# Order, spacing and queues of the last output stores of an attention and MLP kernel

## The chip, the core and the metric

The kernel runs on one core of a Trainium2 chip. Its time is the device time of one execution in microseconds (us), measured on the chip. The engines are TensorE (PE in the profile; its weight loads are shown apart as PEld), VectorE (DVE), ScalarE (ACT), GpSimd (POOL) and SyncE (SP), which here only issues transfers (DMAs). Each engine works through its own queue in order and waits at semaphores for the others. "Issue" of a DMA is the time its engine spends on starting it; it "lands" later, when the last of its 16 completion counts has arrived.

## What is computed

The input x has 2048 rows of 512. It is normalised row by row, goes through an attention with 32 heads of 16 that works in four segments of 512 rows and carries a memory from segment to segment, and through an MLP with a hidden width of 1792. Both results are added to x.

```python
xn = _layernorm(x, axis=-1)
return x + _A_ref(xn, A_wq, A_wk, A_wv, A_wo, A_beta) + _B_ref(xn, B_w1, B_w2)

# _A_ref, for each segment s (qs, ks, vs: its 512 rows, per head)
p = _softmax(logits, axis=-1)                 # causal within the segment
a_dot = jnp.einsum('bhqk,bhkd->bhqd', p, vs)
num = jnp.einsum('bhld,bhde->bhle', pq, M)    # pq = phi(qs), M and z from earlier segments
den = jnp.einsum('bhld,bhd->bhl', pq, z)[..., None] + 1e-06
o = g * (num / den) + (1.0 - g) * a_dot       # all heads together, then o @ wo

# _B_ref
h = _silu(jnp.einsum('bsd,df->bsf', x, w1))
out = jnp.einsum('bsf,fd->bsd', h, w2)
```

## The kernel before

All five engines run from one order written out by hand: the string ORDER (lines 16 to 98) is a list of words, and the loop at line 795 turns each word into the instructions of one piece of work, in that order. Each engine's queue gets its instructions in the order of the words. PIECES (line 759) says which function a word calls. The words that matter here, with s the segment (0 to 3), are:

- S (line 653): a batch of attention scores and their exponentials, the last being S78; E and O (line 687) weigh the values, Ev and Oa copy the results out of PSUM (lines 716 and 722). Oa issues four small DMAs that carry sums of the weights to the tile zraw and four that complete the tile oraw (lines 708 and 730).
- R, W (lines 519 and 527): reciprocals of the sums, for the last segment in two parts; r, w do this for the memory's sums.
- z and d (lines 548 and 558): two DMAs each that spread such reciprocals over all rows (spread, line 536, issue at 542). zv and dv multiply by them, n is a product with the memory's state (line 566), nv adds it and completes one of four slices of the tile oT (line 570).
- o3.j.i (line 593): one product of output tile j (128 rows of 512) of the last segment with contraction step i. Steps 0 to 13 take the MLP's hidden tile hT and w2, steps 14 to 17 take the four slices of oT and wo. oc is half of such a product in columns, od a quarter. Eighteen steps complete a tile.
- oh.i.h (line 625): the same for tile 3 of the last segment, which is made in two halves of 256 columns, each in a PSUM bank of its own. Tile 2 and the two halves lie in one PSUM tile of four banks (fin, an instance of psS), which is free when the last scores have been read. Tiles 0 and 1 have a bank each from the pool pb, which has four.
- st3.j (line 639, store at 581): when all products of a tile are in, VectorE forms 0.5 times the sum plus the residual row tile (line 586) and SyncE stores the 128 KB result (line 591). sh.h (line 628) does it for a half of tile 3, 64 KB (lines 633 and 637). These are called output passes below.
- xl3.j (line 576): SyncE loads the residual tile of x that the pass adds (line 579).

A product has two forms (line 317): whole, one matmul of 128 output rows, or narrow, four matmuls of 32 output rows each that run side by side. The loop chooses by what stands ahead, so that TensorE does not change its form too often; after the last scores all products are narrow.

TensorE works in the order of the words, so a tile's pass comes as soon as its last product is in and VectorE reaches it. The order of the five last passes is tile 0, half 0, tile 2, tile 1, half 1. All stores of the kernel go out from SyncE's queue, in which the spreads, the moves and the residual loads stand too. The pass of tile 1 of segment 2 (st2.1) stands in S78 ahead of the last weighing. ScalarE issues four DMAs in the whole kernel, all of them loads: two of x at the start, w2 and wo.

Of the kernel before, what the change touches and what calls it, by code (L numbers as in the profile page):

```python
# [91 lines left out]
S73 h3.2.1 ha3.2 Ev14 oc2.2.5.1 o2.1.2 o2.2.16 o2.1.6 hv3.12 h3.8.0 o2.2.10 st2.2 hv3.2 o2.1.1 o2.1.5 h3.8.1 ha3.8 hv3.8  # L92
S79 o2.1.0 O14 Ov14 od2.1.12.2 s3 sv3 r3.1 o2.1.7 r3.3 h3.7.0 r3.2 r3.0 oc2.1.10.0 od2.1.12.3 o2.1.3 w3
S77 h3.6.0 R0.0 oc2.1.11.0 h3.7.1 R0.1 ha3.7 h3.6.1 hv3.7 d3.2 o2.1.14 R0.3 h3.9.0 ha3.6 hv3.6 o2.1.15
S76 o2.1.8 d3.0 d3.1 h3.9.1 o2.1.9 oc2.1.10.1 h3.13.0 ha3.9 od2.1.12.0 oc2.1.11.1 h3.13.1 xl3.3 hv3.9 o3.0.12 od2.1.12.1 o2.1.4 o3.0.1 o2.1.13 ha3.13
S75 dv3.2 R0.2 W0 o3.0.7 hv3.13 o3.0.4 h3.10.0 z3.2 o2.1.16 h3.10.1 z3.1 o3.0.2 o3.0.8 dv3.0 o3.0.9 o3.0.0 z3.0 ha3.10 hv3.10
S78 o3.0.5 h3.11.0 o2.1.17 st2.1 h3.11.1 E15 o3.0.6 o3.2.1 oh1.1 o3.1.8 Ev15 ha3.11 oc3.0.3.1 oh0.1 O15 oh12.1 o3.2.3 o3.2.5 hv3.11 zv3.1 oh5.1 o3.2.8 n3.2 Oa15 oh13.0 o3.1.3 o3.1.12 dv3.1 zv3.2 nv3.2 o3.2.7 oc3.0.11.1 oc3.0.11.0 oh9.0 n3.0 oh16.0 n3.1 zv3.0 o3.2.9 o3.1.1 oc3.1.0.1 o3.1.13 o3.2.0 oc3.1.0.0 o3.2.12 o3.2.6 nv3.0 od3.1.11.2 nv3.1 oh11.1 o3.1.14 oh15.1 o3.2.11 oh0.0 R1.1 R1.0 oh10.0 o3.0.14 od3.0.10.2 oh8.0 od3.1.11.3 d3.3 oh15.0 od3.0.10.0 R1.3 o3.1.6 R1.2 oc3.1.9.0 oc3.1.9.1 o3.1.5 oh2.0 o3.1.10 W1 oh14.0 o3.2.13 oh1.0 o3.1.15 oh5.0 o3.0.15 o3.0.16 dv3.3 z3.3 od3.0.10.1 o3.2.15 xl3.1 o3.2.16 zv3.3 o3.2.2 n3.3 oh11.0 od3.1.11.1 oh3.1 oh10.1 oh6.0 oh4.1 nv3.3 o3.1.4 od3.0.10.3 oh4.0 oh12.0 o3.2.4 o3.0.13 oc3.0.3.0 oh3.0 o3.0.17 xl3.0 st3.0 o3.2.14 od3.1.11.0 oh7.0 o3.2.17 oh17.0 oh7.1 sh0 o3.2.10 o3.1.2 oh2.1 o3.1.7 o3.1.16 st3.2 o3.1.17 oh17.1 st3.1 oh6.1 oh13.1 oh14.1 oh16.1 oh8.1 oh9.1 sh1
"""


# [1 line left out]
def kernel(  # L102
# [13 lines left out]
    nc = tc.nc  # L116

    P = 128
# [3 lines left out]
    NT = S // P  # L122
# [11 lines left out]
    out_flat = out.flatten_outer_dims()  # L134
# [40 lines left out]
    def load_w(eng, w_sb, W, k0, k1):  # L175
# [11 lines left out]
        out=beta_r[:], in_=bass.AP(tensor=A_beta.tensor, offset=A_beta.offset, ap=[[1, H], [0, 4], [1, 1]])  # L187
# [9 lines left out]
    for i in range(2):  # L197
# [6 lines left out]
        out=b16[:], in_=ones8[:], compare_op=ALU.is_ge, fill=0.0,  # L204
# [3 lines left out]
        out=b16[:], in_=b16[:], compare_op=ALU.is_ge, fill=0.0,  # L208
# [271 lines left out]
    LAST = NSEG - 1  # L480
# [100 lines left out]
    def store(s, j):  # L581

        st = sts[s]
        t = s * TPS + j
        o_out = work.tile([P, D], BF16, name="o_out", bufs=3)
        out = nc.vector.scalar_tensor_tensor(  # L586
            out=o_out[:], in0=st.pop(("psO", j)), scalar=0.5, in1=st["x", j][:], op0=ALU.mult, op1=ALU.add
        )
        if s == LAST and j >= 2:
            fin_out.append(((j,), out))  # L590
        nc.sync.dma_start(out=out_flat[t * P : (t + 1) * P, :], in_=o_out[:])

    def out_mm(s, j, i, half=None, part=0, parts=1):

# [33 lines left out]
    def half_store(h):  # L628

        st, j, cols = sts[LAST], TPS - 1, slice(h * D // 2, (h + 1) * D // 2)  # L630
        assert len(st.pop(("done", j, h))) == 4 * (FT + DT)
        o_half = work.tile([P, D // 2], BF16, name="o_half", bufs=2)
        out = nc.vector.scalar_tensor_tensor(
            out=o_half[:], in0=st["psO", j, h], scalar=0.5, in1=st["x", j][:, cols], op0=ALU.mult, op1=ALU.add
        )
        fin_out.append(((j, h), out))
        nc.sync.dma_start(out=out_flat[(NT - 1) * P : NT * P, cols], in_=o_half[:])

    def out_store(s, j):
        assert len(sts[s].pop(("done", j))) == 4 * (FT + DT)  # L640
        store(s, j)
# [111 lines left out]
    def keep_busy(n):  # L753
# [20 lines left out]
        "o": out_mm, "oh": half_out,  # L774
        "oc": lambda s, j, i, c: out_mm(s, j, i, None, c, 2), "od": lambda s, j, i, c: out_mm(s, j, i, None, c, 4),
        "sh": half_store, "xl": load_res, "st": out_store,
        "xs": ln_stats, "xc": ln_sums, "xd": ln_var, "xg": ln_root, "xq": ln_sqrt, "xi": ln_inv, "tb": first_exp,
        "Nv": lambda t: ln_norm(t, nc.vector), "Na": lambda t: ln_norm(t, nc.gpsimd),
# [55 lines left out]
```

## Time and profile before

| what | value |
|---|---|
| time, median of 3 runs | 228.55 us (228.1 to 229.02) |
| time of the profiled execution | 229.09 us |
| span of the profiled execution, first to last instruction | 227.4 us |
| TensorE busy | 217.2 us, 96% |
| ScalarE busy | 198.0 us, 87% |
| VectorE busy | 177.7 us, 78% |
| GpSimd busy | 113.9 us, 50% |
| stores of 128 KB (line 591) | 15, issued 87.3 to 224.0 us after the start |
| last issues of a residual load (line 579) | 217.56 us and 218.06 us |
| issues of SyncE between 196.8 and 218.5 us | 34 DMAs |

The profile is of one execution. A row of a timeline names the start, the duration, the engine, the line, the operation and the tiles, written as output<-input, and how many instructions are merged in it; what stands in brackets is the idle time ahead of it and what ended it. A busy TensorE is one with a matmul in flight; the ends of matmuls are modelled. The view by stage gives the busy time of each engine in a stretch, with its instructions, the granted clock (1.00 is full speed) and the share of the DMA engines. The chain of waits goes back from the end, at each step to what released it.

### The profile page before, as it was taken

The page shows a single profiled execution, that of the slowest core. Times are in us where ns is not written, and L with a number is a line of the kernel's source. Part 1 is how long each engine was busy: PE and PEld are TensorE (multiplying, and loading weights), DVE is VectorE, ACT ScalarE, POOL GpSimd, SP SyncE. Part 2 cuts the span into 40 slices and gives each one's busy share as a digit, 9 for nine tenths or more (in the row PEclk, how much of TensorE's full clock was granted, in tenths as well). Part 3 has the DMA queues.
Part 4 walks back from the last instruction along what each step waited for, and adds up shares of the span by engine and source line. Part 5 has one row for each costly group of instructions (what it writes and reads, how often), then busy time and mean ns, then how long its engine had stood idle before and what let it go on. Part 6 is the DMA issues. An engine that isn't in the chain of part 4 may idle for free.

```text
span 227.4 us, 7543 instructions
## 1 busy us (share of the span) xinstructions
PE 217.2 (96%) x3124; PEld 112.9 (50%) x3152; DVE 177.7 (78%) x351; ACT 198.0 (87%) x179; POOL 113.9 (50%) x173
## 2 busy tenths in 40 slices
PE   8999999999999999999999999999999999999993
PEld 8666645545534434444444434445444444445662
DVE  5799899987787897658798798747676888887834
ACT  3799998999999999999999899999999989897000
POOL 6059647667454673665644577546474265342000
PEclk9999999999999999999999999999999999999999
DMA  6992429323215213404314212141032212024122
GB/s 181 361 381 68 77 52 299 60 55 57 61 22 158 72 35 47 96 15 112 41 40 113 75 53 58 35 117 42 22 100 66 88 36 84 29 63 130 29 90 94
DMA packets 34787, 20.55 MB, mean 90 GB/s; under 512 B 15680, under 2 KB 34240, under 8 KB 34752
## 3 DMA queue, kind: packets, MB, share of 16 engines
q1 hardware_dynamic: 32128, 17.45, 28.3%
q10 hardware_dynamic: 2624, 2.62, 3.6%
q8 instruction: 24, 0.39, 0.8%
q14 instruction: 11, 0.09, 0.1%
HBM read 9.96 MB, written 2.10 MB: 53 GB/s over the span
## 4 chain that ended last, share of the span: by engine, by line
PE 62%; ACT 11%; DVE 11%; DMA 8%; issue 4%; SPq 2%; POOL 0%; DVEq 0%
PE ps L322 18%; PE psO L322 14%; PE psS L662 9%; ACT Pb L669 8%; PE ps L324 8%; PE psO L324 6%; PE psV L696 6%; DMA x_hi<-in_A_x_dram 4%; DMA spr<-rz 3%; ACT th L457 2%; DMA x_res<-in_A_x_dram 2%; DVE stats L272 1%; DVE o_out L586 1%; DVE kT L361 1%; PE psM L324 1%
## 5 line engine op out<-in xcount | busy, mean ns | idle before, releaser
L669 ACT ACTIVATE Pb<-psS 128x2048 bf16<-128x2048 f32 x80 | 150.2, 1878 | 5.8 <-PE psS L662 5.1
L677 POOL TENSOR_SCALAR_AFFINE_SELECT Pb<-Pb 128x512 bf16<-128x512 bf16 (+1 forms) x112 | 80.1, 729 | 85.1 <-ACT Pb L669 83.7
L462 DVE SCALAR_TENSOR_TENSOR hT<-th,ps 128x512 bf16<-128x512 bf16 x56 | 37.8, 679 | 14.1 <-ACT th L457 13.7
L322 PE MATMUL ps<-xnT,w_sb 128*128 128x512 bf16 (+1 forms) x177 | 43.3, 340 | 0.8 <-issue 0.5
L322 PE MATMUL psO<-w_sb,hT 128*128 128x512 bf16 (+2 forms) x139 | 36.1, 340 | 0.7 <-issue 0.5
L457 ACT ACTIVATE th<-ps 128x512 bf16<-128x512 f32 x56 | 32.8, 597 | 0.5 <-PE ps L322 0.4
L324 PE MATMUL psO<-w_sb,hT 128*32 128x128 bf16 (+2 forms) x468 | 26.7, 300 | 0.0
L322 PEld LDWEIGHTS <-w_sb 128*128 128x128 bf16 x184 | 17.1, 98 | 16.3 <-issue 3.3
L696 PE MATMUL psV<-Pb,Vz 128*32 128x128 bf16 (+3 forms) x512 | 23.1, 300 | 0.4 <-DVE oT L573 0.2
L322 PEld LDWEIGHTS <-hT 128*128 128x128 bf16 x149 | 13.6, 97 | 16.9 <-issue 4.8
L324 PE MATMUL ps<-xnT,w_sb 128*32 128x512 bf16 (+1 forms) x384 | 21.8, 329 | 0.0
L324 PEld LDWEIGHTS <-hT 128*32 128x32 bf16 x636 | 15.7, 97 | 9.7 <-issue 1.7
L696 PEld LDWEIGHTS <-Vz 128*32 128x32 bf16 x512 | 13.0, 96 | 10.6 <-issue 1.4
L662 PE MATMUL psS<-qT,kT 16*128 16x128 bf16 (+3 forms) x256 | 17.3, 301 | 0.9 <-ACT Pb L669 0.8
L662 PE MATMUL psS<-qT,kTo 32*128 32x384 bf16 (+3 forms) x256 | 17.2, 299 | 0.6 <-ACT Pb L669 0.2
L362 POOL TENSOR_SCALAR kTo<-kT,pm_odd 128x512 bf16<-128x512 bf16 x16 | 11.9, 747 | 8.2 <-DVE kT L361 7.3
L322 PE MATMUL ps<-xnT,wk_sb 128*128 128x512 bf16 (+1 forms) x66 | 15.4, 328 | 0.7 <-issue 0.5
L322 PE MATMUL ps<-wv_sb,xnT 128*128 128x512 bf16 x48 | 14.3, 380 | 0.6 <-issue 0.2
L662 PEld LDWEIGHTS <-kT 16*128 16x128 bf16 x256 | 5.9, 91 | 16.7 <-issue 16.2
L361 DVE CAST kT<-ps 128x512 bf16<-128x512 f32 x15 | 10.2, 687 | 4.6 <-PE ps L322 4.3
L586 DVE SCALAR_TENSOR_TENSOR o_out<-psO,x_res 128x512 bf16<-128x512 f32 x14 | 9.6, 687 | 5.3 <-PE psO L322 2.8
L719 DVE CAST oraw<-psV 128x512 bf16<-128x512 f32 x16 | 11.0, 688 | 3.4 <-PE psV L696 3.3
(105 smaller groups left out, 298.3 us busy)
## 6 DMA issues: line engine op xcount, KB each, us to landing
spr<-rz SPq DMA_DIRECT2D x56, 64.0 KB
x_res<-in_A_x_dram SPq DMA_DIRECT2D x16, 128.0 KB
out_dram<-o_out SPq DMA_DIRECT2D x15, 128.0 KB
w_sb<-in_B_w_dram SPq DMA_DIRECT2D x1, 1792.0 KB
w_sb<-in_B_w_dram ACTq DMA_DIRECT2D x1, 1792.0 KB
x_hi<-in_A_x_dram SPq DMA_DIRECT2D x2, 512.0 KB
oraw<-odd SPq DMA_DIRECT2D x64, 16.0 KB
wv_sb<-in_A_wv_dram SPq DMA_DIRECT2D x2, 256.0 KB
```

What stands on the lines that cost most here:

```text
L322: return [nc.tensor.matmul(out, lhsT=lhsT, rhs=rhs, start=start, stop=stop, skip_group_check=True)]
L324: nc.tensor.matmul(out[c : c + 32], lhsT=lhsT[:, c : c + 32], rhs=rhs, start=start, stop=stop, tile_position=(0, c), skip_group_check=True,)
L361: copy(out=kT[:, dt, :], in_=sts[s].pop(("k", dt))[:, :])
L362: nc.gpsimd.tensor_scalar(out=kTo[:, dt, :], in0=kT[:, dt, :], scalar1=pm_odd[:, 0:1], scalar2=1.0, op0=ALU.mult, op1=ALU.mult,)
L457: nc.scalar.activation(out=th[:], in_=sts[s]["h", ft][:, :], func=AF.Tanh, scale=0.5)
L462: nc.vector.scalar_tensor_tensor(out=st["hT"][:, ft, :], in0=st.pop(("th", ft))[:], scalar=1.0, in1=st.pop(("h", ft))[:, :], op0=ALU.add, ...
L586: out = nc.vector.scalar_tensor_tensor(out=o_out[:], in0=st.pop(("psO", j)), scalar=0.5, in1=st["x", j][:], op0=ALU.mult, op1=ALU.add)
L662: nc.tensor.matmul(psS[:, g, c0 : c0 + nq], lhsT=kk[rows, dt, kt * P : (kt + 1) * P], rhs=st["qT"][rows, dt, kt * P : L], start=True, stop ...
L669: exp = nc.scalar.activation(out=Pb[:, :, :], in_=psS[:, :, :], func=AF.Exp, scale=SCALE)
L677: mask = nc.gpsimd.affine_select(out=blocks, in_=blocks, compare_op=ALU.is_ge, fill=0.0, base=0, pattern=[[0, blocks.shape[1]], [1, P]], c ...
L696: nc.tensor.matmul(psV[32 * g : 32 * g + 32, kt * P : L], lhsT=Vzs[s % 2][:, kt, 4 * dt + g, par : par + 2, :].rearrange("p a d -> p (a d) ...
L719: copy(out=oraw[:], in_=sts[s].pop(("psV", 0))[:, :])
```

## The change

Two issue calls choose their queue, and the order of the last section is written anew. Nothing is computed in another way, and each product of the last segment is still formed once.

- The store of tile 2 of the last segment and the store of half 0 of tile 3 are issued from ScalarE's queue and not from SyncE's.
- The order of the five last passes becomes half 1, half 0, tile 0, tile 2, tile 1. Products of tile 1 fill the end: after half 1's pass come one product of tile 2 and then only products of tile 1 (a half, a quarter and four whole ones, and at last another half).
- Products of the halves (oh) begin earlier and end earlier. The MLP's hidden tiles 10 and 11 (h3.10, h3.11) come earlier by some words. The last slice of oT (d3.3, z3.3, n3.3, nv3.3) keeps its chain, but n3.3 stands nearer to the first product that reads it.
- st2.1 moves from ahead of the last weighing (E15) to after the last spread's issue: its store now stands in SyncE's queue between the residual loads of tiles 1 and 0.
- The reciprocals R1 stand ahead of nv3.1 and not behind it in VectorE's queue.

```diff
 S77 h3.6.0 R0.0 oc2.1.11.0 h3.7.1 R0.1 ha3.7 h3.6.1 hv3.7 d3.2 o2.1.14 R0.3 h3.9.0 ha3.6 hv3.6 o2.1.15
-S76 o2.1.8 d3.0 d3.1 h3.9.1 o2.1.9 oc2.1.10.1 h3.13.0 ha3.9 od2.1.12.0 oc2.1.11.1 h3.13.1 xl3.3 hv3.9 o3.0.12 od2.1.12.1 o2.1.4 o3.0.1 o2.1.13 ha3.13
-S75 dv3.2 R0.2 W0 o3.0.7 hv3.13 o3.0.4 h3.10.0 z3.2 o2.1.16 h3.10.1 z3.1 o3.0.2 o3.0.8 dv3.0 o3.0.9 o3.0.0 z3.0 ha3.10 hv3.10
-S78 o3.0.5 h3.11.0 o2.1.17 st2.1 h3.11.1 E15 o3.0.6 o3.2.1 oh1.1 o3.1.8 Ev15 ha3.11 oc3.0.3.1 oh0.1 O15 oh12.1 o3.2.3 o3.2.5 hv3.11 zv3.1 oh5.1 o3.2.8 n3.2 Oa15 oh13.0 o3.1.3 o3.1.12 dv3.1 zv3.2 nv3.2 o3.2.7 oc3.0.11.1 oc3.0.11.0 oh9.0 n3.0 oh16.0 n3.1 zv3.0 o3.2.9 o3.1.1 oc3.1.0.1 o3.1.13 o3.2.0 oc3.1.0.0 o3.2.12 o3.2.6 nv3.0 od3.1.11.2 nv3.1 oh11.1 o3.1.14 oh15.1 o3.2.11 oh0.0 R1.1 R1.0 oh10.0 o3.0.14 od3.0.10.2 oh8.0 od3.1.11.3 d3.3 oh15.0 od3.0.10.0 R1.3 o3.1.6 R1.2 oc3.1.9.0 oc3.1.9.1 o3.1.5 oh2.0 o3.1.10 W1 oh14.0 o3.2.13 oh1.0 o3.1.15 oh5.0 o3.0.15 o3.0.16 dv3.3 z3.3 od3.0.10.1 o3.2.15 xl3.1 o3.2.16 zv3.3 o3.2.2 n3.3 oh11.0 od3.1.11.1 oh3.1 oh10.1 oh6.0 oh4.1 nv3.3 o3.1.4 od3.0.10.3 oh4.0 oh12.0 o3.2.4 o3.0.13 oc3.0.3.0 oh3.0 o3.0.17 xl3.0 st3.0 o3.2.14 od3.1.11.0 oh7.0 o3.2.17 oh17.0 oh7.1 sh0 o3.2.10 o3.1.2 oh2.1 o3.1.7 o3.1.16 st3.2 o3.1.17 oh17.1 st3.1 oh6.1 oh13.1 oh14.1 oh16.1 oh8.1 oh9.1 sh1
+S76 o2.1.8 d3.0 d3.1 h3.9.1 o2.1.9 oc2.1.10.1 h3.13.0 ha3.9 od2.1.12.0 oc2.1.11.1 h3.13.1 xl3.3 hv3.9 o3.0.12 ha3.13 o3.0.8 R0.2 o2.1.17 o3.0.6 o3.0.2 o2.1.4
+S75 o3.0.9 h3.11.0 hv3.13 h3.10.0 o2.1.16 h3.10.1 o2.1.13 o3.0.0 oc3.0.3.0 ha3.10
+S78 od2.1.12.1 W0 h3.11.1 z3.0 dv3.0 o3.0.1 hv3.10 E15 o3.0.4 ha3.11 od3.0.10.1 dv3.2 oc3.0.3.1 z3.1 z3.2 Ev15 o3.0.13 o3.0.5 oh4.0 o3.2.12 oh0.0 oh2.1 hv3.11 zv3.0 oh5.1 od3.0.10.0 O15 dv3.1 oh3.1 oh7.1 n3.0 zv3.1 oh6.1 o3.2.13 Oa15 oh6.0 oh12.0 od3.0.10.3 o3.1.13 d3.3 o3.1.1 nv3.0 o3.1.8 oh3.0 n3.2 od3.0.10.2 o3.2.10 oh0.1 o3.1.3 zv3.2 o3.2.8 oh8.0 nv3.2 R1.1 oh13.1 oh10.1 od3.1.11.1 o3.0.7 oh16.0 R1.2 oh16.1 oh14.0 oc3.1.9.1 R1.3 R1.0 oh14.1 oh13.0 oh2.0 o3.1.16 o3.1.12 oh9.0 o3.2.0 o3.1.10 o3.2.7 oh1.1 n3.1 oh5.0 o3.1.2 oh10.0 o3.1.6 o3.1.4 W1 o3.2.9 oh12.1 nv3.1 oc3.1.0.1 z3.3 xl3.1 oh7.0 od3.1.11.0 o3.0.14 o3.2.14 oh8.1 oc3.0.11.0 st2.1 dv3.3 zv3.3 o3.0.16 o3.2.4 o3.2.11 o3.2.2 oh11.0 oh15.0 oh9.1 n3.3 oh15.1 xl3.0 o3.1.5 oh11.1 oh4.1 nv3.3 o3.2.15 oh1.0 o3.0.15 oh17.1 od3.1.11.2 o3.2.16 oh17.0 oc3.0.11.1 o3.2.1 o3.2.3 o3.0.17 o3.2.5 o3.2.17 sh1 o3.2.6 o3.1.15 oc3.1.9.0 od3.1.11.3 sh0 o3.1.7 st3.0 o3.1.17 o3.1.14 st3.2 oc3.1.0.0 st3.1
...
-        nc.sync.dma_start(out=out_flat[t * P : (t + 1) * P, :], in_=o_out[:])
+        (nc.scalar if s == LAST and j == 2 else nc.sync).dma_start(out=out_flat[t * P : (t + 1) * P, :], in_=o_out[:])
...
-        nc.sync.dma_start(out=out_flat[(NT - 1) * P : NT * P, cols], in_=o_half[:])
+        (nc.sync if h else nc.scalar).dma_start(out=out_flat[(NT - 1) * P : NT * P, cols], in_=o_half[:])
```

## The prediction

> **What bounds the kernel now.** I read the busy time by stage first, because the change acts on the end alone. Up to the word o3.0.12 of the order the instruction streams are the same; what differs starts near 203 us.
>
> ```profile
> core 0: us, PE busy (x) PEld busy (x) DVE busy (x) ACT busy (x) POOL busy (x), PEclk, DMA share, GB/s
> 210.00:215.00 5.00, 5.00 (x128) 3.12 (x120) 4.21 (x10) 0.59 (x1) 0.00 (x0) 1.00 0.16 43
> 215.00:220.00 5.00, 5.00 (x148) 3.45 (x144) 2.52 (x7) 0.00 (x0) 0.00 (x0) 1.00 0.37 111
> 220.00:223.50 3.50, 3.50 (x96) 2.30 (x88) 1.98 (x5) 0.00 (x0) 0.00 (x0) 1.00 0.06 18
> 223.50:227.40 3.90, 0.10 (x4) 0.00 (x0) 0.80 (x2) 0.00 (x0) 0.00 (x0) 1.00 0.38 122
> ```
>
> TensorE works without a hole at full clock until 223.5, then 3.9 us pass in which it does nothing. So the time is TensorE's stream plus that tail. The timeline of TensorE gives the stream's pace and two places that matter below:
>
> ```profile
> 218.49 0.39 PE L324 MATMUL ps<-phiQT,Mbf 128*32 128x512 bf16 x4
> 220.44 0.39 PE L324 MATMUL psO<-wo_sb,oT 128*32 128x512 bf16 x4
> 223.21 0.39 PE L324 MATMUL psS<-w_sb,hT 128*32 128x256 bf16 x8
> ```
>
> A product (four matmuls side by side in the narrow form) starts 0.216 us after the one before at 512 columns, 0.109 at 256, 0.056 at 128; a 512-column one is done 0.39 us after its start, a 256-column one 0.28 (starts and ends in this timeline). From 203 us on, the starts leave these intervals only at the four edges of the two last score batches, by about 0.1 us each. The last product starts at 223.32 and is done at 223.60. VectorE, SyncE's queue and the chain of waits give the tail:
>
> ```profile
> 219.53 0.69 DVE L573 TENSOR_TENSOR oT<-ps,oT 128x512 bf16<-128x512 f32 x1
> 221.75 0.69 DVE L586 SCALAR_TENSOR_TENSOR o_out<-psO,x_res 128x512 bf16<-128x512 f32 x1 [1.52 <-PE psS L324]
> 222.35 0.41 DVE L633 SCALAR_TENSOR_TENSOR o_half<-psS,x_res 128x256 bf16<-128x256 f32 x1
> 222.69 0.68 DVE L586 SCALAR_TENSOR_TENSOR o_out<-psS,x_res 128x512 bf16<-128x512 f32 x1
> 223.28 0.68 DVE L586 SCALAR_TENSOR_TENSOR o_out<-psO,x_res 128x512 bf16<-128x512 f32 x1
> 223.88 0.41 DVE L633 SCALAR_TENSOR_TENSOR o_half<-psS,x_res 128x256 bf16<-128x256 f32 x1
> ```
>
> ```profile
> 217.56 0.93 SPq L579 DMA_DIRECT2D x_res<-in_A_x_dram  x2
> 222.47 0.34 SPq L591 DMA_DIRECT2D out_dram<-o_out  x1
> 222.91 0.38 SPq L637 DMA_DIRECT2D out_dram<-o_half  x1
> 223.41 0.92 SPq L591 DMA_DIRECT2D out_dram<-o_out  x2
> 224.77 0.34 SPq L637 DMA_DIRECT2D out_dram<-o_half  x1
> ```
>
> ```profile
> 218.06 3.60 DMA x_res<-in_A_x_dram
> 221.75 0.53 DVE o_out L586
> 222.35 0.41 DVE o_half L633
> 222.77 1.19 DVE o_out L586 x2
> ```
>
> Read together: the first output pass waited for its residual load, which landed at 221.65, 3.60 us after issue; its neighbour of the same size took 2.26. From then on the five passes follow each other with no hole (0.60 us from start to start for a full one, 0.33 for a half), so VectorE and not TensorE ends the work: the last pass starts 0.28 us after its product is done and ends at 224.30. Its store is issued only at 224.77, although SyncE was free at 224.33. By the completion counts in the trace it lands at 226.53; the end follows 0.85 later, at 227.38. The tail after the last product's start is thus 0.98 (to the end of the pass) + 0.47 (to the issue) + 1.76 (to landing) + 0.85 = 4.06.
>
> **The change part by part.**
> *TensorE's amount of work.* The order holds the same products; three matmuls fewer (one product falls into the whole form). The same score batches, so the same four edges. Cost 0, as long as TensorE never waits (first rival).
>
> *The passes closed in the order half 1, half 0, tile 0, tile 2, tile 1.* The pass of half 1 waits for the product just ahead of it in the order, o3.2.17 (it lies in the same PSUM tile). Up to the last product (tile 1's, 256 columns) come then o3.2.6 and six products of tile 1, so o3.2.17 starts 6 x 0.216 + 0.109 + 0.056 = 1.46 us before that one, itself counted. With the stream's end where it is, it starts at 223.32 - 1.46 = 221.86 and is done at 222.25; the pass starts about 0.05 later (the row at 207.60 starts 0.03 behind its product, others to 0.05), at 222.30. Behind it, at VectorE's own pace: half 0 at 222.63, tile 0 at 222.96, tile 2 at 223.56, tile 1 at 224.16; it ends at 224.84. Tile 1's product is done at 223.60, so VectorE binds again, by 0.5 us: one half pass that stood last has become a full one, and it starts later. Against 224.30 this is +0.54. The residual loads hide: the last wanted one is now read at 222.96, so the 1.3 us by which one came late has cover; without the cover it was worth about 0.25 here.
>
> *The last store's issue.* The 0.37 us in which SyncE stood free ahead of its last store has two like it in its own stream, 0.45 near 71.4 and 0.39 near 150.6, and the three lie 128 SyncE instructions apart. With two stores and two waits gone to ScalarE, the last store stands two places ahead of the next such place, and the hole falls behind it, where SyncE waits for landings anyway. So the issue follows the pass by 0.03, as with tile 1's store at 223.99: 224.87 instead of 224.77. The two bounds are 0 and 0.37 for the hole; I take 0, by the equal distances. The Trainium skill (Runtime: NRT & Kernel Launch, Instruction fetch mechanics) says that instructions come in 16 KiB blocks of 256 and that crossing a boundary is mostly hidden; by that nothing would happen at 128, and the hole would be something else that may stay. The trace shows 8,192-byte packets of the instruction queue and a distance of 128, so I go by the trace.
>
> *ScalarE's two issues.* ScalarE is done at 210.7, so nothing waits behind them. No store from it is in this trace; its loads take 0.38 to 0.46 to issue, SyncE's last stores 0.33 to 0.38. Tile 2's store, issued about 224.27, would land near 226.1, some 0.5 ahead of the last one. So issuing from there is worth between 0 and 0.1 us lost, hidden: 0. SyncE would have been free in time as well, its issues being 0.34 against passes 0.60 apart. The Trainium skill (DMA: Bandwidth & Descriptors, Issuing engines are not separate DMA queues) says that issuing from a second engine saves only the issuing time; by that rule too the two moved stores bring nothing themselves, which speaks against the change.
>
> *Landing.* The last store is 128 KB and no longer 64. Full stores landed 1.73, 1.74 and 1.80 after issue in this trace, halves 1.59 and 1.76. I take 1.76, bounds 1.73 and 1.80.
>
> *The delayed store of segment 2* leaves SyncE's queue ahead of the sums (0.40 us at 209.07) and comes back between the two residual loads. What comes behind it, tile 0's load, has 2 us of cover.
>
> Sum on the profiled execution: 224.84 + 0.03 + 1.76 + 0.85 = 227.48, against 227.38: +0.10. Its time is 229.09, its span 227.38, so 1.71 lie around; that run is 0.54 above the median 228.55. Most of that can be the late residual load: without it the passes would follow the products, the last starting at 223.65, and the store would go out at 224.39, 0.38 earlier. The changed kernel doesn't have this loss to give back. So the change costs 0.10 where every run has the late load, and 0.10 + 0.38 = 0.48 where only the profiled one had: 228.65 to 229.03. I take 228.8.
>
> **The rivals.**
> *TensorE waits for the last slice of oT (slower).* Its 512-column product with the state starts at 218.49 and the first reader at 220.44, 1.95 later. In the new order 4.32 - 0.11 = 4.21 us of products follow that product's start and 2.92 follow the reader's, so there are only 1.29 between them. Needed are 0.39 (product) + 0.05 + 0.69 (pass at 219.53) + 0.14 (wait and weight load) = 1.27. So it just fits if the spread for the slice lands at 218.98 or before. SyncE should issue it about 0.3 us earlier, since the reciprocals no longer stand behind a pass of oT (0.7) and the queue then binds. From there each late us is a us at the end. Transfers did come late in this stage, by 1.3 to 1.7 us: a spread landed 3.75 after issue where 2.07 is usual, a move 3.53 where 1.8 is, the residual load; 16 KB instruction packets of 0.9 to 1.4 us start at 209.5, 214.9 and 219.5. The spread would move at 216.5 to 218.6, between two of them, which speaks against. If one hits, 1.6 - 0.3 = 1.3 is lost: 230.1.
>
> *VectorE keeps up (faster).* If the passes followed the products and not each other, tile 1's would start at 223.65 and end at 224.33, 0.5 sooner: 228.1 to 228.5. Against it speaks the fixed 0.60 between passes in three pairs here. Even so nothing over 0.5% comes out.
>
> *The hole stays* ahead of the last store: +0.37, 229.2.
>
> *A gain upstream* would have to come out of TensorE's stream, which has 0.4 us of edges left after 203: no more than that, 228.4; a larger one needs something that this trace doesn't show, 227.3.
>
> **How the numbers follow.** Forecast, with its own range 228.3 to 229.4: 0.56. The hole stays: 0.10. VectorE keeps up, or a small gain upstream: 0.10. TensorE waits: 0.16. The larger gain: 0.08. About 0.5%, 1.14 us, can be told from no change; the bounds are 227.41 and 229.69. Faster 0.08, the larger gain alone; slower 0.16, the wait of TensorE; the other cases are the same, 0.76. The range 227.9 to 229.9 holds all but the far ends of these two.
>
> **What would show it.** TensorE busy to within 0.2 us of 223.5, and no hole ahead of the first products with the last slice; five passes back to back, the last a full one starting 0.5 us behind its product; SyncE's last issue within 0.1 us of that pass's end; its 128 KB landing last, after ScalarE's. A weight load of oT that waits near 220.3, a spread that takes over 3 us, or a hole of 0.37 ahead of the last issue would make it wrong.

## The result and the profile after

The changed kernel takes 229.15 us (median, 228.37 to 232.84, 22 runs) beside 228.5 us (227.87 to 230.96, 22 runs) for the kernel before on the same chip: a ratio of 1.0046, 95% interval 1.0027 to 1.0064, some 1.05 us. A comparison leaves out runs more than 1.5% above their kernel's fastest; here that is the one at 232.84.

The runs fall into two groups. Fourteen lie between 228.37 and 229.62, median 228.90, which is 0.40 above the kernel before. Seven lie between 230.57 and 231.27, median 230.99, 2.1 above the others. Of the kernel before only one run in 22 is above 230.3. The two groups together give 0.40 + 7/21 x 2.1 = 1.1 us, which is the difference measured. So there are two things to explain: a small loss in every run, and a large one in a third of them.

The profiled execution of the changed kernel is its fastest run, 228.37 us with a span of 226.66, and stands for the first group. (That of the kernel before is above its median, at 229.09; the chains of exponentials in the two were 0.9 us apart at 157 us already, where both execute the same work. So I compare times from the last product's start, 222.46 here and 223.33 before.) The busy time by stage:

```profile
core 0: us, PE busy (x) PEld busy (x) DVE busy (x) ACT busy (x) POOL busy (x), PEclk, DMA share, GB/s
215.00:220.00 5.00, 5.00 (x136) 3.56 (x132) 2.83 (x5) 0.00 (x0) 0.00 (x0) 1.00 0.46 134
220.00:223.50 3.50, 2.73 (x64) 1.48 (x55) 2.07 (x5) 0.00 (x0) 0.00 (x0) 1.00 0.14 41
223.50:226.70 3.20, 0.00 (x0) 0.00 (x0) 0.47 (x1) 0.00 (x0) 0.00 (x0) 0.99 0.37 126
```

TensorE is busy without a hole until 222.73, and 3.9 us follow in which it does nothing, as before. Its timeline at the places that the prediction named (the product with the state, the first reader of the last slice, the last product), and VectorE's:

```profile
218.22 0.40 PE L324 MATMUL ps<-phiQT,Mbf 128*32 128x512 bf16 x4
219.51 0.30 PE L324 MATMUL psS<-wo_sb,oT 128*32 128x256 bf16 x4
222.44 0.30 PE L324 MATMUL psO<-w_sb,hT 128*32 128x256 bf16 x4
```

```profile
218.03 0.42 DVE L554 TENSOR_TENSOR oT<-spr,oraw 128x512 bf16<-128x512 bf16 x1 [0.95 <-DMA spr<-rz]
218.66 0.69 DVE L573 TENSOR_TENSOR oT<-ps,oT 128x512 bf16<-128x512 f32 x1 [0.21 <-PE ps L324]
221.43 0.76 DVE L633 SCALAR_TENSOR_TENSOR o_half<-psS,x_res 128x256 bf16<-128x256 f32 x2 [2.07 <-PE psS L324]
222.10 0.68 DVE L586 SCALAR_TENSOR_TENSOR o_out<-psO,x_res 128x512 bf16<-128x512 f32 x1
222.70 0.68 DVE L586 SCALAR_TENSOR_TENSOR o_out<-psS,x_res 128x512 bf16<-128x512 f32 x1
223.29 0.68 DVE L586 SCALAR_TENSOR_TENSOR o_out<-psO,x_res 128x512 bf16<-128x512 f32 x1
```

The reader starts 1.29 us after the product with the state, and the pass that completes the slice (line 573) ends at 219.35, 0.16 ahead of it: the slice comes just in time. The five output passes stand without a hole; the last starts 0.83 after the last product's start and 0.56 after that product is done. The two queues that issue the stores, and the end of the chain of waits:

```profile
221.88 0.34 SPq L637 DMA_DIRECT2D out_dram<-o_half  x1
222.81 0.34 SPq L591 DMA_DIRECT2D out_dram<-o_out  x1
224.00 0.33 SPq L591 DMA_DIRECT2D out_dram<-o_out  x1
```

```profile
222.21 0.37 ACTq L637 DMA_DIRECT2D out_dram<-o_half  x1
223.41 0.36 ACTq L591 DMA_DIRECT2D out_dram<-o_out  x1
```

```profile
217.43 0.97 PE psS L324 x24
...
222.18 1.20 DVE o_out L586 x2
```

The last store goes out 0.03 after its pass and lands 1.80 later, at 225.80 by its completion counts; the end follows 0.85 after that. The residual load is gone from the end of the chain, which goes from the products straight to VectorE's passes.

### The profile page after: what moved, and what is told of

Read it like the earlier page. It is cut to its first block, busy times and chain, and to the rows that moved or that the text cites. A ratio compares the mean times of both kernels' runs of the same rounds, so it can differ in the third digit from the quotient of the medians.

```text
span 226.7 us, 7564 instructions
## 1 busy us (share of the span) xinstructions
PE 219.7 (97%) x3149; PEld 113.2 (50%) x3149; DVE 177.2 (78%) x351; ACT 198.1 (87%) x179; POOL 114.0 (50%) x173
## 4 chain that ended last, share of the span: by engine, by line
PE 72%; ACT 12%; DVE 6%; DMA 3%; issue 3%; SPq 1%; POOL 0%; DVEq 0%
PE ps L322 19%; PE psO L322 15%; PE psS L662 9%; PE psO L324 9%; ACT Pb L669 9%; PE ps L324 8%; PE psV L696 6%; DMA x_hi<-in_A_x_dram 3%; PE psS L324 3%; ACT th L457 2%; DVE stats L272 1%; DVE kT L361 1%; PE psM L324 1%; SPq L176 1%; ACT ex L395 1%
## 5 line engine op out<-in xcount | busy, mean ns | idle before, releaser
L677 POOL TENSOR_SCALAR_AFFINE_SELECT Pb<-Pb 128x512 bf16<-128x512 bf16 (+1 forms) x112 | 79.1, 720 | 84.7 <-ACT Pb L669 83.4
L322 PE MATMUL ps<-xnT,w_sb 128*128 128x512 bf16 (+1 forms) x186 | 45.4, 342 | 0.0
L322 PE MATMUL psO<-w_sb,hT 128*128 128x512 bf16 (+2 forms) x147 | 38.8, 343 | 0.0
L324 PE MATMUL psO<-w_sb,hT 128*32 128x128 bf16 (+2 forms) x476 | 27.7, 301 | 0.0
L324 PE MATMUL ps<-xnT,w_sb 128*32 128x512 bf16 (+1 forms) x376 | 21.2, 328 | 0.0
L324 PEld LDWEIGHTS <-hT 128*32 128x32 bf16 x644 | 16.6, 97 | 9.1 <-issue 1.7
L362 POOL TENSOR_SCALAR kTo<-kT,pm_odd 128x512 bf16<-128x512 bf16 x16 | 12.4, 774 | 8.0 <-DVE kT L361 7.0
L322 PE MATMUL ps<-xnT,wk_sb 128*128 128x512 bf16 (+1 forms) x69 | 16.1, 330 | 0.0
L322 PE MATMUL ps<-wv_sb,xnT 128*128 128x512 bf16 x53 | 15.6, 380 | 0.2
L726 DVE CAST odd<-psV 128x512 bf16<-128x512 f32 x15 | 10.3, 687 | 3.7 <-PE psV L696 3.6
```

What stands on the lines that cost most here:

```text
L322: return [nc.tensor.matmul(out, lhsT=lhsT, rhs=rhs, start=start, stop=stop, skip_group_check=True)]
L324: nc.tensor.matmul(out[c : c + 32], lhsT=lhsT[:, c : c + 32], rhs=rhs, start=start, stop=stop, tile_position=(0, c), skip_group_check=True,)
L362: nc.gpsimd.tensor_scalar(out=kTo[:, dt, :], in0=kT[:, dt, :], scalar1=pm_odd[:, 0:1], scalar2=1.0, op0=ALU.mult, op1=ALU.mult,)
L677: mask = nc.gpsimd.affine_select(out=blocks, in_=blocks, compare_op=ALU.is_ge, fill=0.0, base=0, pattern=[[0, blocks.shape[1]], [1, P]], c ...
L726: copy(out=odd[:], in_=sts[s].pop(("psV", 1))[:, :])
```

## The experiments

Eleven kernels ran in three groups, each group on one chip beside the kernel before. In the table "high" counts the runs above 230.3 us, out of those compared.

| kernel | median us | high | ratio to the kernel before | interval |
|---|---|---|---|---|
| kernel before (four comparisons) | 228.4 to 228.8 | 3 of 121 | 1 | |
| changed kernel | 229.15 | 7 of 21 | 1.0046 | 1.0027 to 1.0064 |
| 1 old order, two stores from ScalarE | 227.81 | 0 of 12 | 0.9975 | 0.9956 to 0.9994 |
| 2 new order, all stores from SyncE | 229.36 | 4 of 12 | 1.0044 | 1.0012 to 1.0076 |
| 3 changed, more slack for the last slice | 229.0 | 2 of 12 | 1.0025 | 0.9999 to 1.0051 |
| 4 changed kernel again | 229.55 | 3 of 12 | 1.0044 | 1.0016 to 1.0073 |
| 5 changed, 16 KB packet later | 229.32 | 1 of 12 | 1.0014 | 0.9989 to 1.0040 |
| 6 changed, 16 KB packet earlier | 230.37 | 6 of 12 | 1.0059 | 1.0028 to 1.0090 |
| 7 changed, early passes | 228.44 | 1 of 10 | 1.0003 | 0.9965 to 1.0041 |
| 8 as 1, late loads from ScalarE | 228.74 | 0 of 12 | 0.9987 | 0.9960 to 1.0014 |
| 9 as 1, those loads 24 us earlier | 227.83 | 0 of 12 | 0.9970 | 0.9948 to 0.9993 |
| 10 as 1 | 228.06 | 0 of 12 | 0.9989 | 0.9970 to 1.0008 |
| 11 changed, with 3, 5 and 7 together | 228.47 | 0 of 12 | 0.9999 | 0.9978 to 1.0020 |

### 1 and 2: the queues and the order apart

The first keeps the old order and takes only the two queues from the change; the second takes only the order.

```diff
 # 1, on the kernel before
-        nc.sync.dma_start(out=out_flat[t * P : (t + 1) * P, :], in_=o_out[:])
+        (nc.scalar if s == LAST and j == 2 else nc.sync).dma_start(out=out_flat[t * P : (t + 1) * P, :], in_=o_out[:])
...
-        nc.sync.dma_start(out=out_flat[(NT - 1) * P : NT * P, cols], in_=o_half[:])
+        (nc.sync if h else nc.scalar).dma_start(out=out_flat[(NT - 1) * P : NT * P, cols], in_=o_half[:])
 # 2, on the changed kernel: the same two lines the other way round
```

> The old order; only the stores of tile 2 and of half 0 go out from ScalarE. Theory of the hole (an instruction block of SyncE ends ahead of its last store): SyncE's stream is four instructions shorter, the hole of 0.37 us falls behind the last store, so the profile shows the last issue within 0.1 us of the last pass's end and the time falls by 0.3 to 0.4 us (ratio 0.9983 to 0.9987). Rival: a second issuing queue saves nothing here and the hole is something else: ratio 1.000, hole still there. No group of runs near 231 us, since the order of the last slice is the old one.

> The new order, all stores from SyncE. If the queues bring nothing in the new order, it equals the changed kernel: about 228.9 us with a second group of runs near 231, ratio 1.002 to 1.007. By its place in SyncE's stream the hole lies ahead of tile 2's store and delays that store alone, so the last store is not later. Rival: the second queue carries the new order, and without it the last store is later by 0.34 or more in every run.

The order alone costs as much as the whole change (1.0044 against 1.0046), and has the same high runs. The queues alone, in the old order, come out faster, by 0.25% here (0.13 to 0.17% was expected) and by 0.11% in the repetition (10), whose interval still holds 1. SyncE's queue at the end of the first shows how:

```profile
224.53 0.34 SPq L591 DMA_DIRECT2D out_dram<-o_out  x1
224.99 0.35 SPq L637 DMA_DIRECT2D out_dram<-o_half  x1
```

The pass of the last half ends at 224.83 and its store goes out at 224.99, held only by the store ahead of it (224.53 to 224.87). The hole of 0.37 us that stood here in the kernel before has moved behind the last store (225.49 to 225.86), where SyncE waits for landings. In the second kernel, which has SyncE's two stores and two waits back, the hole is back too, but ahead of the last store but one:

```profile
223.35 0.37 SPq L591 DMA_DIRECT2D out_dram<-o_out  x1
...
224.15 0.34 SPq L591 DMA_DIRECT2D out_dram<-o_out  x1
...
224.59 0.37 SPq L591 DMA_DIRECT2D out_dram<-o_out  x1
```

The middle row is tile 2's store: its pass ended at 223.92, SyncE was free at 223.72, and it went out 0.23 after the pass. The last store's issue, 0.07 after its pass (224.52), hardly feels it. So in the new order the second queue brings nothing that the times show.

One thing beside the hole differs in the profiles. In the old order the last store landed 1.76 us after issue with all stores on SyncE (kernel before), and 1.53 to 1.57 with two on ScalarE (1, 8, 9, 10). In the new order it took 2.00 with all on SyncE (2), and 1.69 to 1.80 otherwise. With one profile in each order that has all stores on SyncE it is not shown that the queue does this.

### 3 and 4: is it the last slice?

The third kernel moves the two products of the halves that read the last slice of oT first, so that its first reader comes later. The fourth is the changed kernel once more, beside it.

```diff
-... o3.0.15 oh17.1 od3.1.11.2 o3.2.16 oh17.0 oc3.0.11.1 o3.2.1 o3.2.3 o3.0.17 o3.2.5 o3.2.17 sh1 ...
+... o3.0.15 od3.1.11.2 o3.2.16 oc3.0.11.1 o3.2.1 o3.2.3 o3.2.5 oh17.1 oh17.0 o3.0.17 o3.2.17 sh1 ...
```

> The new order with the two half products of the last slice of oT moved four products later, so that 2.3 us instead of 1.3 lie between the state product and the first reader. Theory (the runs near 231 are those in which the spread of the last reciprocals lands late and TensorE waits): the main group stays at 228.9, the upper group falls by 1.0 us to about 230 or vanishes, the ratio falls to 1.001 to 1.003. Rival (the upper group comes from something else, for instance the passes or the stores): the two groups stay as they are, ratio 1.0046.

> The changed kernel once more, for a second profile and more runs. Theory: again most runs near 228.9 and about a third near 231; if the profile falls into the upper group, it shows the spread of z3.3 landing 1.5 us or more later than 2.07 after its issue and TensorE idle by about 2 us ahead of its first product with the last slice. Rival: the upper runs are longer somewhere else, ahead of 200 us.

In the third kernel four runs stand apart, at 229.89 to 230.40, where the four of the changed kernel beside it lie at 230.06 to 231.36: slack lowers them and does not remove them. The fourth kernel's profiled execution happened to be one of the high runs (230.91 us, span 229.2), and shows what they are. Chain of waits, VectorE and TensorE:

```profile
216.46 4.28 DMA spr<-rz
...
224.80 1.19 DVE o_out L586 x2
```

```profile
220.85 0.43 DVE L554 TENSOR_TENSOR oT<-spr,oraw 128x512 bf16<-128x512 bf16 x1 [3.17 <-DMA spr<-rz]
221.38 0.69 DVE L573 TENSOR_TENSOR oT<-ps,oT 128x512 bf16<-128x512 f32 x1
225.91 0.68 DVE L586 SCALAR_TENSOR_TENSOR o_out<-psO,x_res 128x512 bf16<-128x512 f32 x1
```

```profile
219.60 0.40 PE L324 MATMUL psO<-wo_sb,oT 128*32 128x512 bf16 x4
222.13 0.29 PE L324 MATMUL psS<-wo_sb,oT 128*32 128x256 bf16 x4 [2.13 <-DVE oT L573]
```

The second transfer of the last slice's spread takes 4.28 us from issue to landing instead of 2.06 (a spread has 9 completion counts in the traces; the last of them is taken). VectorE waits 3.17 us for it, TensorE 2.13 for VectorE, and all that follows is the tail of the undisturbed run, moved back. This is the rival "TensorE waits for the last slice of oT" of the prediction.

The packets of this transfer tell what held it. Each of a spread's two transfers moves 128 packets of 512 bytes. Here 112 of the second's came in their place, at 217.70 to 218.11, and 16 only at 219.31 to 220.14. In the same stretch stands a 16 KB packet of TensorE's instruction queue, from 218.45 to 219.33: the 16 come when it ends. The 13 profiles of this case record some 700 transfers of this kind. In 19 of them 112 packets came in their place and 16 were missing from it; by each of the 19 stands a 16 KB packet, which overlaps the transfer (17 times) or starts within 0.4 us behind it (2 times). In 64 transfers such a packet overlaps and nothing is missing, and in 67 more one starts within 0.4 us behind and nothing is missing. None of the 567 transfers without a packet near it misses any. So an overlap holds a transfer up about one time in five, a packet that starts behind it hardly ever (2 of 69).

### 5 and 6: the 16 KB packet moved

The packets follow the count of TensorE's instructions (176 to 309 apart, 250 on average, over the last five distances of the changed kernel's profile). So the same work in fewer or more instructions, far ahead, shifts the packets in time and leaves the last section as it is.

```diff
 # 5: two products in quarters made whole, 48 instructions fewer
-S47 q3.2.1 d1.1 oc1.0.4.1 od1.0.5.0 vv3.1 od1.0.5.2 o1.0.12 hv1.7 od1.0.5.1 od1.0.5.3 dv1.2 ...
+S47 q3.2.1 d1.1 oc1.0.4.1 vv3.1 o1.0.12 hv1.7 o1.0.5 dv1.2 ...
-... od2.2.6.1 n2.0 zv2.0 od2.2.6.3 ... od2.2.6.0 o2.2.4 od2.2.6.2
+... n2.0 zv2.0 ... o2.2.4 o2.2.6
 # 6: five whole products made in halves, 40 instructions more
-... o2.0.9 ... o2.0.12 ... o2.0.15 ... o2.2.9 ... o2.2.17 ...
+... oc2.0.9.0 oc2.0.9.1 ... oc2.0.12.0 oc2.0.12.1 ... oc2.0.15.0 oc2.0.15.1 ... oc2.2.9.0 oc2.2.9.1 ... oc2.2.17.0 oc2.2.17.1 ...
```

> The changed kernel, with two products of segments 1 and 2 that were done in four parts done whole: 48 TensorE instructions fewer ahead of the last section, the same work. At the 37 instructions per us of the last stage, TensorE's 16 KB instruction packet that stood 4.3 to 5.1 us ahead of the last product should come about 1.3 us later, near -3.4, when the spread for the last slice (landed by about -4.5) is through. Theory (that packet, when it meets the spread, holds back part of it; this makes the runs near 231): no run or one in twelve above 230.3, median 228.7 to 229.0, ratio 1.000 to 1.0025. Rival (the spread is held by something else in the order, for instance the residual loads issued behind it): a third of the runs near 231 as before, ratio 1.004 to 1.005.

> The changed kernel, with five whole products of segment 2 done in two parts each: 40 TensorE instructions more ahead of the last section, the same work. The 16 KB packet should come about 1.1 us earlier, near -5.8 from the last product, right across the two transfers of the last slice's spread (second issue at -6.5, packets from about -5.4). Theory: at least as many runs near 231 as in the changed kernel, a third to all, ratio 1.004 to 1.009. Rival (not the packet): a third as before, with the kernel with the later packet showing a third too.

With the packet later, one run of 12 is above 230.3 (and one at 230.19); with it earlier, six are, and eight above 229.8. The profile of the sixth kernel caught a meeting:

```profile
220.77 0.43 DVE L554 TENSOR_TENSOR oT<-spr,oraw 128x512 bf16<-128x512 bf16 x1 [2.52 <-DMA x_res<-in_A_x_dram]
```

```profile
222.04 0.29 PE L324 MATMUL psS<-wo_sb,oT 128*32 128x256 bf16 x4 [1.82 <-DVE oT L573]
```

(The view names the residual load behind the spread as the releaser. That load landed at 220.99, after the row's start, and line 554 reads spr and oraw only; the spread landed at 220.64.) The packet records of the profiles, in us:

```
                        second transfer of the last spread   16 KB packet       TensorE waits
changed kernel          217.09 to 217.50, 128 packets        217.76 to 219.19   no
2 all stores SyncE      217.63 to 218.05, 128 packets        218.26 to 219.73   no
3 more slack            218.95 to 219.37, 128 packets        218.18 to 219.44   0.15
4 changed again         217.70 to 218.11, 112; 16 late       218.45 to 219.33   2.1
5 packet later          218.38 to 218.79, 128 packets        219.89 to 220.90   0.2
6 packet earlier        218.26 to 218.67, 112; 16 late       217.40 to 218.85   1.8
7 early passes          218.45 to 218.87, 128 packets        219.07 to 220.34   no
kernel before           218.16 to 218.58, 128 packets        219.47 to 220.40   no
```

In the sixth kernel both transfers of the spread miss 16 packets, and those 32 come from 218.83 on, as the packet ends. So in both high runs that were profiled, 4 and 6, the instruction packet goes with the held spread, and the held spread with TensorE's wait. For the other high runs this is argued: their counts (1 of 12 with the packets later, 10 of 33 unchanged, 6 of 12 with them earlier) fit, but are too few to show it alone.

Why a third of the runs is high stays open. In the old order's five profiles the packet starts 0.22 to 1.10 us after the spread's last packet (0.68 on average), in four of the new order's with the packet where the change left it 0.20 to 0.34, with experiment 5 at 1.10. That is nearer, but at such a distance only 2 of 69 transfers were held; the high runs without a profile may have had other distances.

The third kernel's profile shows a second way to a late slice. There the packet ahead (213.82 to 215.16) met SyncE's last move of oraw:

```profile
213.71 1.83 SPq L730 DMA_DIRECT2D oraw<-odd  x1
```

The issue took 1.83 us where 0.59 is usual, and the spread was issued some 1.2 late. Its own packet overlapped it and held nothing. (The 0.15 of the table is the product with the state, which waited for the slice's other spread.) With this kernel's slack the slice came in time for its first reader (complete at 221.15, read at 221.33). With the changed kernel's 1.29 us TensorE would have waited about 0.9, an estimate: the product with the state starts at 219.00, the reader would be due at 220.29 and could start at 221.20. In the high runs too an issue ahead of the spread was held beside that packet: its first transfer in the fourth (0.99 us where 0.67 is usual), a move in the sixth (1.23). By the same sum this makes about 0.1 of the 2.3 us by which the reader starts late in the fourth, and 0.4 of 2.0 in the sixth. Experiments 5 and 6 move all of TensorE's packets and do not keep the two ways apart.

One more thing is seen in the fifth. Its spread was not met, and yet TensorE waited 0.2 us: SyncE had issued it late, and the reader's 1.29 us leave little for that. Its undisturbed runs lie no lower than the changed kernel's (the ten up to 229.74 have a median of 229.2).

### 7: the 0.4 us of the undisturbed runs

```diff
-... oh17.0 oc3.0.11.1 o3.2.1 o3.2.3 o3.0.17 o3.2.5 o3.2.17 sh1 o3.2.6 ... od3.1.11.3 sh0 o3.1.7 st3.0 o3.1.17 ...
+... oh17.0 sh1 sh0 oc3.0.11.1 o3.2.1 o3.2.3 o3.0.17 st3.0 o3.2.5 o3.2.17 o3.2.6 ... od3.1.11.3 o3.1.7 o3.1.17 ...
```

> The changed kernel, with the passes of the two halves and of tile 0 written right behind their own last products in the order; products and queues as they were. Theory (VectorE's five passes back to back at the end are the 0.4 us that the undisturbed runs of the changed kernel lie above the kernel before): the last pass starts about 0.05 behind its product and ends 0.5 earlier; undisturbed runs 228.2 to 228.6; the runs near 231 stay as frequent and fall a little; ratio 1.001 to 1.003. Rival (the 0.4 us lie upstream of the tail, TensorE's stream ends later): ratio 1.004 to 1.005.

```profile
224.14 0.69 DVE L586 SCALAR_TENSOR_TENSOR o_out<-psO,x_res 128x512 bf16<-128x512 f32 x1 [0.45 <-PE psO L324]
```

VectorE is now idle for 0.45 us ahead of the last pass, which starts 0.32 after the last product's start (223.82) where it was 0.83. The runs below 229.2 have a median of 228.3, against 228.9 for the changed kernel in both its measurements and for experiment 5 on the same chip: 0.6, of which the tail gives 0.5. So the loss in every run is VectorE's five passes back to back. The high runs stay: one at 231.43 in the comparison, and two above its bound, at 232.3 and 232.4. Without these two the ratio, 1.0003, comes out below the 1.001 to 1.003 expected.

### 8 to 11: what is left to gain

The eighth and ninth kernels take the residual loads of tiles 1 and 0 out of the last spread's neighbourhood, in the old order with the two stores on ScalarE's queue. The eighth issues them from ScalarE's queue behind Oa15. The ninth issues them from SyncE's at 193, into buffers that are dead by then.

```diff
 # 8 (the words xl3.1 xl3.0 moved to behind Oa15)
+        (nc.scalar if s == LAST and j < 2 else nc.sync).dma_start(out=sts[s]["x", j][:], in_=x_flat[t * P : (t + 1) * P, :])
 # 9 (the words moved to behind Ev14)
+        sts[s]["x", j] = work.tile([P, D], BF16, name="x_res", tag="pk" if s == LAST and j < 2 else "x_res", bufs=4)
```

> The kernel before in its order, with the two stores on ScalarE's queue as in the first experiment, and the last two residual loads issued from ScalarE's queue too, some 10 us earlier, right behind its last copy of a product. Theory (a residual load of 3.6 to 3.8 us holds the first output pass, and the five passes that follow back to back carry 0.25 to 0.4 us of it to the end): first output pass waits for its product only, last pass ends 0.25 to 0.4 earlier, ratio 0.995 to 0.997. Rival (the load's lateness is made up by the gaps behind it): ratio 0.9975 as with the two stores alone.

> The kernel before in its order, the two stores on ScalarE's queue as in the first experiment, and the last two residual loads issued by SyncE some 24 us earlier (near 194, where its queue is idle), into buffers that held pk and are dead by then. Theory (the residual loads' lateness was worth 0.4 us in the tail of the first experiment; loads issued at 209.8 from ScalarE's queue gave it back because they stood ahead of the last sums' moves): output passes follow their products, last pass about 0.05 behind its product, last issue right behind it, nothing changed upstream; ratio 0.994 to 0.9965. Rival (the tail is not what decides): 0.9975 as the first experiment.

> The first experiment once more, beside the other two on one chip: ratio 0.9965 to 0.9985, with no run near 231.

> The changed kernel with the three edits together: the slack for the last slice (third experiment), the 48 fewer TensorE instructions ahead (fifth) and the early output passes (seventh). Theory (the changed kernel's loss is TensorE's wait for the last slice in a third of the runs, and five passes back to back in the others): both gone, runs 228.0 to 228.6 without an upper group, ratio 0.997 to 0.9995. Rival (something else of the order costs time): ratio above 1.0005.

The eighth failed. Its tail is as expected (last pass 0.06 behind its product, store right behind it), but TensorE waited twice in the chain of the last slice:

```profile
218.63 0.40 PE L324 MATMUL ps<-phiQT,Mbf 128*32 128x512 bf16 x4 [0.33 <-DVE phiQT L564]
...
221.17 0.40 PE L324 MATMUL psO<-wo_sb,oT 128*32 128x512 bf16 x4 [0.39 <-DVE oT L573]
```

SyncE's last move of oraw took 1.22 us to issue (213.94 to 215.16) where 0.6 is usual, beside a 16 KB packet at 213.87 to 214.79. Whether the loads at 209.8 had a part in it, one profile cannot tell. The ninth is the fastest kernel of the study, 0.9970, and with the first the only one whose interval lies below 1. It falls short of the 0.994 to 0.9965 expected and cannot be told from the tenth, which ran beside it. The tenth's profile says why. Here the residual loads landed 2.13 and 2.27 us after issue, not 3.78 and 3.61 as in the first kernel's profile, and the passes follow their products:

```profile
220.74 0.69 DVE L586 SCALAR_TENSOR_TENSOR o_out<-psO,x_res 128x512 bf16<-128x512 f32 x1 [0.92 <-PE psO L324]
...
223.51 0.43 DVE L633 SCALAR_TENSOR_TENSOR o_half<-psS,x_res 128x256 bf16<-128x256 f32 x1
```

The last pass ends 0.76 after the last product's start (223.18); in the first kernel's profile, with the late loads, 1.14. So the late residual load costs 0.38 us, and not in every run: in the first a 16 KB packet starts at 219.32, when both loads are under way (landed 221.87 and 222.19); in the tenth it starts at 219.27, as the first load lands (219.28).

The eleventh takes on both losses of the changed kernel and comes out level with the kernel before (0.9999, where 0.997 to 0.9995 was expected), with no run above 230.3. It does not reach the first kernel: its last pass ends 1.09 after the last product's start, 0.33 more than the tenth's: a full pass stands last, 0.27 us longer than a half, and VectorE still binds a little.

## Why the prediction was right, and where it was not

The time came out 0.35 us above the point, inside the range, and "the same" by the bound of 0.5% is right, though only just (the interval reaches 0.64%). There is luck in it: the median stays inside because only a third of the runs wait. With six in 12, as in experiment 6, it stands at 230.37, outside. By its steps:

- *TensorE's amount of work: 0.* Right in two thirds of the runs. In the profiled one no product of the last section waits.
- *The passes.* Right to 0.01. Predicted from the last product's start: -1.02, -0.69, -0.36, +0.24 and +0.84; measured: -1.03, -0.69, -0.36, +0.24 and +0.83. Experiment 7 shows that this is what the undisturbed runs lose.
- *The last store's issue.* Right: 0.03 after the pass. Experiments 1 and 2 show that the hole belongs to a place in SyncE's instruction stream; moved by a few instructions, it is at another store.
- *ScalarE's issues: 0.* Right for this order (experiment 2: 1.0044 without them, 1.0046 with). In the old order the same two lines gain, by moving the hole off the last store, and perhaps 0.2 in landing. The rule of the Trainium skill (DMA: Bandwidth & Descriptors, Issuing engines are not separate DMA queues), that a second issuing engine saves issuing time alone, agrees with the new order; the gain in the old one is of another kind.
- *Landing.* 1.80 against 1.76, at the upper bound.
- *The sum.* Predicted 227.48 against 223.33 for the last product, 4.15 after it; measured 226.66 - 222.46 = 4.20. The choice between 0.10 and 0.48, according to how often the kernel before has a late residual load, should have gone to the upper end: undisturbed runs lie 0.40 higher, and experiment 10 shows a run of the old order without the late load, 0.38 shorter in the tail, as computed.

What failed is the weight and the price of the first rival, TensorE's wait for the last slice. It had a chance of 0.16 as a property of the kernel and a price of 1.3 us; it is a property of the run. If all high runs are of the kind of the two profiled ones, it comes in a third of them (10 of 33 runs of the changed kernel) and costs 2.1. One of the forecast's own signs of being wrong, a spread that takes over 3 us, stands in the high run of experiment 4 (4.28). Two steps were wrong:

- "The spread would move at 216.5 to 218.6, between two of them, which speaks against." The packets' times were read as fixed on the clock. They follow TensorE's instruction count. The new order has larger products near the end, so fewer instructions in a microsecond, and they scatter from run to run: between 3.86 and 4.42 us ahead of the last product's start in the old order's profiles, 4.7 to 5.05 in four of the new. The distance of 0.9 us that the profile of before showed was the luck of one run; 0.22 stands in another. Nor was it enough to look at the spread's own transfers: the packet ahead can hold an issue that the spread stands behind, as in experiment 3.
- "If one hits, 1.6 - 0.3 = 1.3 is lost." The spread was 2.2 late (4.28 against 2.06), and the 0.3 by which SyncE was to issue it earlier did not help: in the high run, one issue of the spread ahead of it took 0.99 us where 0.67 is usual, which took the gain back.

The slack was computed well: 1.29 us between product and reader, as measured. Of the 1.27 needed, the 0.14 for wait and weight load is too much: where TensorE did wait, in experiments 4 and 5, the reader starts 0.05 after the pass. So the profiled run of the changed kernel had 0.1 to spare, and not 0.02. A chain with so little to spare, and a transfer in it that is known to come late by 1.3 to 1.7 elsewhere, was the place to put more than a chance of 0.16.

## What to carry to other kernels

Near the end of a kernel, count the slack of each transfer that TensorE will wait for, and compare it with how late transfers of this kind come anywhere in the trace, not with their usual landing: with some 0.1 us of slack a delay that few transfers have cost TensorE 2.1 us where it struck. Times at which instruction packets come move with the instruction count, so a reordering moves them too, and one undisturbed profile says little about it; look at the spread of the runs first, and profile one of each group. Ask of a second queue for stores not what it saves in issuing, but what it moves in the first queue: the gain here was, for the most part that the profiles show, a hole that fell on another instruction.

## What was unexpected of the hardware

- A 16 KB packet of TensorE's instruction queue took 0.88 to 1.62 us. In the changed kernel TensorE ran on beside it without a hole (217.76 to 219.19). It held back 16 of a transfer's 128 packets in 17 of 81 overlaps; where the late ones can be told apart in the records, they come at its end. The Trainium skill (Runtime: NRT & Kernel Launch, Instruction fetch mechanics) says that instructions are fetched in 16 KiB blocks of 256, by the sequencer's own queue, and that the crossing is mostly hidden. Size and distance agree with TensorE's packets here (16,384 bytes, some 250 instructions). Hidden it is for the engine that fetches; for a transfer on the path of another it cost 2.2 us.
- In two of the 19 cases the packet's record begins after the held packets were due (218.45 against 217.70 to 218.11 in experiment 4). What held them until it began is not in the profile.
- SyncE's holes of 0.37 to 0.45 us came every 128 of its instructions, each followed 1.0 to 1.4 us later by a packet of 8,192 bytes, and stood at the same three places of its instruction stream in all 13 profiles. With fewer instructions ahead of the last store, as in experiment 1, that store is issued before the third place. The block of the Trainium skill cited above is twice that.
- Issues can be held too: in experiment 6 a residual load took 1.59 us to issue (217.66 to 219.25) beside the packet at 217.40 to 218.85, where 0.46 is usual, and one move of oraw each in experiments 3, 6 and 8 took 1.83, 1.23 and 1.22 beside such a packet, where 0.59 is usual.
